# Later weight splits in a two-layer expert kernel: moving them from the step before to the first two steps of an expert

## The chip, the cores and the metric

One Trainium2 chip, one NeuronCore. The metric is the device time of one execution in microseconds, the median over several runs.

## The reference, cut to what matters

Attention over 4 batches of 576 positions gives 2304 rows of 512 numbers. Two mixture-of-experts layers follow, each with 8 experts:

```
idx  = argmax(logits, axis=1)          # one expert per row
for e in range(8):
    h = maximum(x[idx == e] @ w1[e], 0)    # 512 -> 1024
    out[idx == e] = gate[:, None] * (h @ w2[e])   # 1024 -> 512
```

Layer 0 has a normalised router with a temperature, layer 1 a plain one on the output of layer 0. The result has float32 accuracy.

## The kernel before, in words

**Steps.** The rows of one expert are gathered into tiles of 128. A layer is a row of steps `t = 0, 1, ...`, one tile each, in the order of the experts: first a large one (its first three tiles are chosen early), then the others, last another large one. Steps from 18 on run under a condition, so that only as many run as there are tiles. One step multiplies its tile with W1 (`ph0`, `ph1`, 12 matmuls each of 128 by 512), evicts, transposes, and multiplies with W2 (`py`, 24 matmuls). A tile of at most 64 rows that ends an expert of two tiles or more (from step 4 on) is a "half step" with fewer matmuls.

**Splits.** TensorE works with fp32r operands, so each weight is split into a high and a low part: ACT writes `Wh` from the staging buffer `stg` (`split_hi`, L909), DVE writes `Wl = stg - Wh` (`split_lo`, L912). A matrix is four chunks, each one operation per engine. `Wh` and `Wl` have two places per matrix: one for the current expert, one for the next. As soon as `stg` has been split, SP reloads it with the expert after the next (`loads`, `dma_chunks`, L1153 and L1155). There is one staging buffer for W1 and one for W2.

**When.** `finish2` computes with small DVE operations, for each expert with first step `s0` and `nt` tiles, the step `st` that its hand-over hangs on: `st = max(s0, 3)` for the first expert, `s0` for the others, and at least 19 for the last expert of layer 0. The next expert's W1 is split late in step `st - 1`, its W2 late in step `st`. The flags lie in two places: `ctl` holds for each step its flags (columns 4 and 5) and which expert to load (columns 0 to 3); `fw` holds the flags of 12 steps as the bits of one number, for steps 4 to 15 and 16 to 27. Steps 2 and 3 read their flags from `ctl` and the weight place from `ini`; the later ones take bits of the two words, which ACT, DVE and POOL load into registers (`words`, L1227) late in steps 2 and 14, ahead of that step's splits.

**Order in a step.** All queues are written out by hand in `step`. Late in a step come: the routing of the previous tile (layer 0, `route2`), the word loads, the splits of W2 and of W1 (L1325 is the condition, `If(self.fv[i] > 0)`), then in layer 0 `place` on DVE (L569 to L579; six tiles in steps 7 and 13, three in 16), the rest of the `py` matmuls, in the last steps of layer 0 `rank_pe`, `rank_ev` and `place` for one tile, and `end`: ACT evicts `py` into `ysb` (L1417). In `end` DVE has a condition of its own (L1426, `If(hv[0] > 0)`) under which it writes `ysb` in a half step.

**What the next step asks of these queues.** Some 3 us into a step, ACT has to evict `ph0` into `hs` (L1481), from which TensorE transposes (L1438). In layer 0, TensorE then transposes the last step's `ysb` (L1368), for which ACT and DVE must have left `end`.

Of the kernel before, what the change touches and what calls it, by code (L numbers as in the profile page):

```python
# [13 lines left out]
ALU = mybir.AluOpType  # L14
# [375 lines left out]
def tile_kernel(ctx, tc, q, k, v, M_prev, z_prev, beta, emb, tau, w1a, w2a, wg, w1b, w2b, out):  # L390
# [43 lines left out]
    k1, ntl = ctile([P, 1], "k1"), ctile([P, 1], "ntl")  # L434
    p17 = ctile([P, 1], "p17")

    TW, BW = NE + 1, 12
    pw = ctile([P, 2], "pw")
    fw = ctile([P, 2, 4], "fw", I32)

# [144 lines left out]
    class Route1:  # L585
# [62 lines left out]
        def rank_ev(self):  # L648
            V = nc.vector
            V.tensor_tensor(out=self.t8, in0=self.o, in1=self.ps, op=ALU.mult)  # L650
            yield
            V.tensor_reduce(out=rkb[:, self.sl], in_=self.t8, axis=AX.X, op=ALU.add)
            yield
# [173 lines left out]
    def finish2(L, st):  # L827
# [10 lines left out]
        ts(out=w["r2"], in0=ract, scalar1=2.0, scalar2=None, op0=ALU.add)  # L838
        ts(out=w["last"], in0=ract, scalar1=kk, scalar2=None, op0=ALU.is_ge)

        stt(out=w["st"], in0=is0, scalar=3.0, in1=s0, op0=ALU.mult, op1=ALU.max)
        V.tensor_tensor(out=c8, in0=ract.unsqueeze(1).to_broadcast([P, E, E]), in1=w["r2"].unsqueeze(2).to_broadcast([P, E, E]), op=ALU.is_equal)

        if L == 0:
# [381 lines left out]
    def words(x, engines):  # L1226
        return list(nc.values_load_multi_w_load_instructions(x, engines=engines, min_val=0, max_val=2 ** BW - 1)[1])  # L1227

    steps = {}
    flag_words, pe_words = {}, {}  # L1230

    class Step:


        def __init__(self, L, t):
            self.L, self.t = L, t
            self.hv, self.lm = None, []
            if 0 < t <= NE:
                self.pv = steps[L, 0].pv
            elif t:  # L1240
                g, k = divmod(t - TW, BW)
                self.words = flag_words[L, g]
                if (L, t) != (0, NT1 - 1):
                    self.hv = [nc.snap((self.words[3] >> k) & 1, engines=[e], min_val=0, max_val=1) for e in (DVE_, ACT_)]
            else:
                self.pv = 0 if L == 0 else nc.values_load(ini[0:1, 1, 4:5], engines=[PE_], min_val=0, max_val=1)
            self.spl = [[], []]
# [12 lines left out]
        def flags(self):  # L1260
            L = self.L
            c = ctl[self.t:self.t + 1, L]
            ld = lambda a, b, e, m: nc.values_load_multi_w_load_instructions(c[:, a:b], engines=e, min_val=0, max_val=m)[1]
            if self.t < TW:
                self.fv = ld(4, 6, [ACT_, DVE_, POOL_], 1)
                self.wv = 1 if L == 0 else nc.values_load(ini[0:1, 1, 5:6], engines=[ACT_, DVE_, POOL_], min_val=0, max_val=1)
            else:
                k = (self.t - TW) % BW
                three = [ACT_, DVE_, POOL_]
                f1, f2, pv = ((w >> k) & 1 for w in self.words[:3])  # L1270
                self.fv = [nc.snap(x, engines=three, min_val=0, max_val=1) for x in (f1, f2)]
                self.wv = nc.snap(1 - pv, engines=three, min_val=0, max_val=1)
            self.cv = ld(0, 2, [SP_], 127)
            self.ev = ld(2, 4, [SP_], E - 1)

        def gemm(self, i, ps, lhs, n0, a, b):

# [43 lines left out]
        def splits(self, i, cs, parts="hl"):  # L1321


            wv = self.wv if i else steps[self.L, self.t + 1].wv
            with tc.If(self.fv[i] > 0):  # L1325
                for c in cs:
                    for x in parts:
                        ins = (split_hi if x == "h" else split_lo)(4 * i + c, wv)
                        for y, d, g in self.spl[i]:
                            if x != y and c != d:  # L1330
                                tc.declare_no_dep(ins, group=g, reason="other chunk")
                        if i:
                            tc.declare_no_dep(ins, group=f"g{i}_{self.L}_{self.t}", reason="other buffer")
                        for mm in last_mm.get(i, ()):
                            tc.add_manual_dep(ins, mm.name, SYNC, reason="buffer free")
                        g = f"{x}{i}_{self.L}_{self.t}_{c}"
                        tc.add_to_no_dep_group(g, ins)
                        self.spl[i].append((x, c, g))
# [120 lines left out]
    def next_flags(L, t):  # L1459
        if t > 2:  # L1460
            steps[L, t].flags()

    def step(L, t):

        s, b = steps[L, t], bufs
        more = 0 < t < NS - 1
        rt2 = L == 0
        late = t >= NT1 - 2
        x = x0 if t == 0 else b.x
        lx = lambda kk: (x, kk)  # L1470
        lh = lambda kk: (b.h[kk // 4], kk % 4)
        begin(L, t)
        if s.hv is None:
            s.gemm(0, ph0, lx, 0, 0, 3)
            yield
            s.gemm(0, ph0, lx, 0, 3, 9)
            yield
            s.gemm(0, ph0, lx, 0, 9, 12)
        else:
            s.either(lambda: s.gemm(0, ph0, lx, 0, 0, 12), lambda: s.gemm2(0, ph0, lx, 0, HQ[0], True))  # L1480
        nc.scalar.activation(out=b.hs[0], in_=ph0, func=AF.Copy)  # L1481
        ahead = (L, t) != (0, NT1 - 1)
        yield
        s.either(lambda: (s.gemm(0, ph1, lx, 512, 0, 6), hT_pe(0, b)), lambda: (s.gemm2(0, ph1, lx, 512, HQ[0][0:4]), hT2_pe(0, b)))
        hT_ev(0, b, s.hv)
        if rt2:
            yT_pe()
            yT_ev(b.hs[0])
        yield
        rk = L == 0 and 2 <= t <= NT1 - 2  # L1490
        if rk:
            rank_pe(t - 2)
            rank_ev(t - 2)
        s.either(lambda: s.gemm(0, ph1, lx, 512, 6, 12), lambda: s.gemm2(0, ph1, lx, 512, HQ[0][4:], True))
        last_mm[0] = s.lm
        nc.scalar.activation(out=b.hs[1], in_=ph1, func=AF.Copy)  # L1496
        yield
        if more:
            xT_pe(rows_of(t + 1))
        if rt2:  # L1500
            parts_pe(b.hs[0])
            parts_ev(b.hs[0])
        if more:
            next_step(L, t + 1)
            hilo(psx, b.x, False, steps[L, t + 1].hv)
        if rt2:
            route2_iov()
        s.either(lambda: (s.gemm(1, py, lh, 0, 0, 3), hT_pe(1, b)), lambda: (s.gemm2(1, py, lh, 0, HQ[1][0:4]), hT2_pe(1, b)))
        hT_ev(1, b, s.hv)
        if more:  # L1510
            next_flags(L, t + 1)
        yield
        if rt2 or s.hv is None:
            s.either(lambda: s.gemm(1, py, lh, 0, 3, 6), lambda: s.gemm2(1, py, lh, 0, HQ[1][4:6]))
        gen = iter(())
        if rt2:
            logits_pe(b.hs[0])
        yield
        if s.hv is None:
            s.gemm(1, py, lh, 0, 6, 9)  # L1520
        if rt2:
            gen = route2(t - 1)
        next(gen, None)
        next(gen, None)
        drain(gen)
        if t == 2:
            s.flags()
        g, k = divmod(t + 2 - TW, BW) if t + 2 < NS else (0, 1)
        if k == 0:
            flag_words[L, g] = words(fw[0:1, g, 0:3], [ACT_, DVE_, POOL_]) + words(fw[0:1, g, 3:4], [ACT_, DVE_])  # L1530
        if not ahead:
            e2.append(nc.values_load(ini[0:1, 1, 0:1], engines=[SP_], min_val=0, max_val=E - 1))
        for i in (1, 0):
            if t > 1 + i and t < NS - 1 + i:
                s.splits(i, range(4))
                s.loads(i, range(4))
        if rk and ((t - 1) % 6 == 0 or t == NT1 - 2):
            c0 = (t - 2) // 6 * 6
            place(c0, t - 1 - c0)
        if s.hv is None:  # L1540
            for q_ in range(9, 24, 3):
                yield
                s.gemm(1, py, lh, 0, q_, q_ + 3)
        else:
            a, n = (6, 6) if rt2 else (3, 4)
            s.either(lambda: s.gemm(1, py, lh, 0, a, 24), lambda: s.gemm2(1, py, lh, 0, HQ[1][n:], True))
        if k == 0:
            pe_words[L, g] = words(fw[0:1, g, 2:4], [PE_])
        if more:
            steps[L, t + 1].pe_flags()  # L1550
        last_mm[1] = s.lm
        if (L, t) == (1, NT1 - 2):

            nc.gpsimd.drain()
        if rt2:
            nc.gpsimd.dma_start(out=x2[P * (t - 1):P * t, DM:XR], in_=xcb)
            if late:
                rank_pe(t - 1)
                rank_ev(t - 1)
                place(t - 1, 1)  # L1560
        if not ahead:

            with tc.If(rg["nt"] <= NT1):
                for c in range(8):
                    for ins in split_chunk(c, rg["wv"]):
                        tc.add_to_no_dep_group("n18", ins)
        end(L, t)

    def abreast(a, b, ns=()):

# [268 lines left out]
```

## Time and profile before

| | us |
|---|---|
| median of 3 runs (lowest to highest) | 903.15 (903.11 to 904.14) |
| the profiled execution | 903.58 |
| its span, first to last instruction | 901.9 |
| TensorE busy | 851.6 (94%) |
| DVE busy | 514.9 (57%) |
| ACT busy | 478.9 (53%) |

PE is the matmul engine TensorE, PEld its weight loads, DVE VectorE, ACT ScalarE, POOL GpSimd, SP the queue that issues most transfers. Matmuls are pipelined, so a row can say that PE is busy though the next matmul started before the last one ended. [...] In the timelines a row has: start, duration, engine, line, operation, tile written and read, shapes, how many in a row, and in brackets how long the engine sat idle before it and what ended that. Register loads, branches and semaphore waits are not rows of a timeline: they show as idle time that ends with "issue" or with a name like ACTq or DVEq (the engine's own sequencer) and a line. A step is taken from its first `ph0` matmul to that of the next.

### The profile page before, as it was taken

The page shows a single profiled execution, that of the slowest core. Times are in us where ns is not written, and L with a number is a line of the kernel's source. Part 1 is how long each engine was busy: PE and PEld are TensorE (multiplying, and loading weights), DVE is VectorE, ACT ScalarE, POOL GpSimd, SP SyncE. Part 2 cuts the span into 40 slices and gives each one's busy share as a digit, 9 for nine tenths or more (in the row PEclk, how much of TensorE's full clock was granted, in tenths as well). Part 3 has the DMA queues.
Part 4 walks back from the last instruction along what each step waited for, and adds up shares of the span by engine and source line. Part 5 has one row for each costly group of instructions (what it writes and reads, how often), then busy time and mean ns, then how long its engine had stood idle before and what let it go on. Part 6 is the DMA issues. An engine that isn't in the chain of part 4 may idle for free. (4 is left out here: it accounts for less than half of the span.)

```text
span 901.9 us, 20713 instructions
## 1 busy us (share of the span) xinstructions
PE 851.6 (94%) x5139; PEld 661.4 (73%) x5139; DVE 514.9 (57%) x1617; ACT 478.9 (53%) x940; POOL 264.0 (29%) x376
## 2 busy tenths in 40 slices
PE   5999999999999999887989999998988999989996
PEld 3777777777777777665868788776877887767785
DVE  4766676576786854676346465744467316363620
ACT  3667667667658244565344543632277426564631
POOL 5457656465451022111121112121112111111111
PEclk9999999999999999987999999999999999999998
DMA  8424454335053454366334116111659415374111
GB/s 131 80 52 95 85 153 114 58 55 113 14 174 109 173 171 150 119 232 210 124 118 144 39 35 206 69 49 39 235 179 337 156 48 181 120 271 143 44 38 40
DMA packets 139826, 110.56 MB, mean 123 GB/s; under 512 B 107258, under 2 KB 107258, under 8 KB 139652
## 3 DMA queue, kind: packets, MB, share of 16 engines
q1 hardware_dynamic: 129252, 85.03, 32.2%
q0 software_dynamic: 8032, 23.22, 7.6%
q8 instruction: 72, 1.18, 0.5%
q14 instruction: 102, 0.84, 0.3%
q10 hardware_dynamic: 2368, 0.30, 0.2%
HBM read 90.32 MB, written 19.25 MB: 121 GB/s over the span
## 5 line engine op out<-in xcount | busy, mean ns | idle before, releaser
L1312 PE MATMUL py<-Wh,b 128*128 (+1 forms) x640 | 221.1, 406 | 0.3 <-ACT hs L1496 0.3
L1312 PE MATMUL ph<-Wh,b 128*128 (+1 forms) x624 | 217.1, 405 | 0.8 <-issue 0.8
L912 DVE TENSOR_TENSOR Wl<-stg,Wh 128x1024 f32 (+1 forms) x120 | 145.7, 1225 | 33.6 <-ACT Wh L909 25.2
L1312 PEld LDWEIGHTS ph<-Wh,b 128*128 128x128 f32 x624 | 119.7, 192 | 29.1 <-issue 3.1
L1208 DVE SCALAR_TENSOR_TENSOR b<-pt,b 128x512 fp32r<-128x512 f32 (+1 forms) x86 | 56.1, 653 | 148.5 <-ACT b L1203 140.5
L1312 PEld LDWEIGHTS py<-Wh,b 128*128 128x128 f32 x640 | 120.2, 188 | 27.8 <-issue 4.7
L909 ACT ACTIVATE Wh<-stg 128x1024 f32 (+1 forms) x120 | 125.7, 1059 | 21.6 <-issue 7.7
L1312 PE MATMUL ph<-Wl,b 128*128 (+2 forms) x336 | 131.7, 398 | 0.0
L1312 PE MATMUL py<-Wl,b 128*128 (+2 forms) x344 | 128.5, 392 | 0.0
L267 ACT ACTIVATE att<-psat 128x512 f32<-128x512 f32 (+1 forms) x144 | 66.5, 462 | 76.0 <-PE psat L265 75.5
L1203 ACT ACTIVATE b<-pt 128x512 fp32r<-128x512 f32 x86 | 51.4, 598 | 85.7 <-PE pt L1438 65.5
L288 PE MATMUL psav<-vb,att 128*128 128x128 f32 (+1 forms) x640 | 93.9, 281 | 0.4 <-ACT att L267 0.2
L288 PEld LDWEIGHTS psav<-vb,att 128*128 128x128 f32 x640 | 80.3, 191 | 17.4 <-ACT att L267 5.6
L1433 POOL DMA_INDIRECT out_dram<-ysb,xca x21 | 22.7, 1083 | 203.4 <-ACT ysb L1417 83.0
L248 ACT ACTIVATE a<-a,mx 128x128 f32<-128x128 f32 (+3 forms) x128 | 71.0, 554 | 5.6 <-DVE mx L213 5.4
L1312 PEld LDWEIGHTS ph<-Wl,b 128*128 128x128 f32 (+1 forms) x336 | 62.0, 184 | 12.1
L1312 PEld LDWEIGHTS py<-Wl,b 128*128 128x128 f32 (+1 forms) x344 | 61.8, 182 | 11.6 <-ACT b L1203 1.0
L213 DVE CUSTOM_DVE_ANT_0 a<-pss,wmask 128x128 f32<-128x128 f32 (+3 forms) x128 | 60.8, 481 | 14.8 <-PE pss L235 14.2
L1438 PE MATMUL pt<-ident,hs 128*128 128x128 f32 x304 | 47.8, 281 | 16.8 <-ACT hs L1481 16.6
L1438 PEld LDWEIGHTS pt<-ident,hs 128*128 128x128 f32 x304 | 37.5, 143 | 31.0 <-ACT hs L1481 22.4
L1168 POOL DMA_INDIRECT xg<-x_scratch,idx x48 | 48.2, 1004 | 37.7 <-issue 16.2
L1417 ACT ACTIVATE ysb<-py,xca 128x512 f32<-128x512 f32 x36 | 24.6, 683 | 62.5 <-PE py L1312 50.9
(389 smaller groups left out, 1253.6 us busy)
## 6 DMA issues: line engine op xcount, KB each, us to landing
stg<-in_moe_w_dram SPq DMA_DIRECT2D x120, 512.0 KB, 8.3
x_scratch<-ysb POOLq DMA_DIRECT2D x22, 256.0 KB, 4.5
qkn<-in_q_dram SPq DMA_DIRECT2D x64, 72.0 KB, 2.4
qkn<-in_k_dram SPq DMA_DIRECT2D x60, 72.0 KB, 2.4
vb<-in_v_dram SPq DMA_DIRECT2D x32, 128.0 KB, 2.4
x_scratch<-xb SPq DMA_DIRECT2D x16, 256.0 KB, 2.9
x_scratch<-stg SPq DMA_DIRECT2D x11, 258.0 KB, 4.1
xg<-x_scratch,idx POOLq DMA_INDIRECT x48, 3.9
```

The source lines that it names most:

```text
L213: nc.vector.tensor_tensor_reduce(out=out, in0=ps, in1=mask, scale=-0.125, scalar=bound, op0=ALU.add, op1=ALU.min, accum_out=m)
L248: nc.scalar.activation(out=a[:, 0:N], in_=a[:, 0:N], func=AF.Exp, scale=-1.0, bias=mx, accum_out=rs_t[pi][:, c, j:j + 1])
L267: nc.scalar.activation(out=att[:, 0:N], in_=ps[:, 0:N], func=AF.Copy)
L288: nc.tensor.matmul(av_t[pi][:, c, j:], att[:, 128 * kb:128 * kb + 128], vn[:, kb, j:, 0:D], start=(kb == 0), stop=(kb == c))
L909: return nc.scalar.activation(out=chunk(Wh, c, wv), in_=stg[:, c].unsqueeze(1), func=AF.Copy).ins
L912: return nc.vector.tensor_tensor(out=chunk(Wl, c, wv), in0=stg[:, c].unsqueeze(1), in1=chunk(Wh, c, wv).bitcast(F32), op=ALU.subtract).ins
L1168: return nc.gpsimd.indirect_dma_start(out=rows_of(t), out_offset=None, in_=rows, in_offset=bass.IndirectOffsetOnAxis(ap=idx[:, L, t:t + 1] ...
L1203: nc.scalar.activation(out=hl[:, :, 0:P], in_=ps, func=AF.Relu if relu else AF.Copy)
L1208: nc.vector.scalar_tensor_tensor(out=o, in0=x, scalar=0.0, in1=h, op0=ALU.max, op1=ALU.subtract)
L1312: mm = nc.tensor.matmul(o, x, W, start=(first and q_ == qs[0]), stop=(last and q_ == qs[-1]))
L1417: whole = lambda: nc.scalar.activation(out=ysb, in_=py, func=AF.Copy, scale=xc[:, 0:1])
L1438: nc.tensor.transpose(pts[i][:, P * kk:P * kk + P], b.hs[i][:, P * kk:P * kk + P], ident)
```

## The change

An expert with three tiles or more gets `st = s0 + 1`: the next expert's W1 is split late in its first step, W2 late in its second, and the loads behind the splits move with them. The first expert's splits (W1 in step 2, W2 in step 3) lose their condition and their flags; the weight place is a constant in layer 0 and one register in layer 1, loaded late in step 16 of layer 0. The bit words cover steps 3 to 15 and 16 to 28, so steps 2 and 3 read no flags from `ctl`; the word loads stand behind the splits of steps 2 and 14. `end` stands ahead of the last steps' `rank_pe`, `rank_ev` and `place`. `finish2` has one DVE operation more.

```diff
-    TW, BW = NE + 1, 12
+    TW, BW = NE, 13
...
-        stt(out=w["st"], in0=is0, scalar=3.0, in1=s0, op0=ALU.mult, op1=ALU.max)
+        stt(out=w["st"], in0=nt, scalar=2.5, in1=s0, op0=ALU.is_gt, op1=ALU.add)
+        stt(out=w["st"], in0=is0, scalar=3.0, in1=w["st"], op0=ALU.mult, op1=ALU.max)
...
-            if self.t < TW:
-                self.fv = ld(4, 6, [ACT_, DVE_, POOL_], 1)
-                self.wv = 1 if L == 0 else nc.values_load(ini[0:1, 1, 5:6], engines=[ACT_, DVE_, POOL_], min_val=0, max_val=1)
-            else:
...
             self.cv = ld(0, 2, [SP_], 127)
             self.ev = ld(2, 4, [SP_], E - 1)
...
+        def split_flags(self):
+            g, k = divmod(self.t - TW, BW)
...
+            self.wv = first_wv[self.L] if self.t <= NE else nc.snap(1 - pv, engines=three, min_val=0, max_val=1)
...
-            wv = self.wv if i else steps[self.L, self.t + 1].wv
-            with tc.If(self.fv[i] > 0):
+            first = self.t == 2 + i
+            wv = first_wv[self.L] if first else self.wv if i else steps[self.L, self.t + 1].wv
+            with ExitStack() if first else tc.If(self.fv[i] > 0):
...
-        g, k = divmod(t + 2 - TW, BW) if t + 2 < NS else (0, 1)
-        if k == 0:
-            flag_words[L, g] = words(fw[0:1, g, 0:3], [ACT_, DVE_, POOL_]) + words(fw[0:1, g, 3:4], [ACT_, DVE_])
...
         for i in (1, 0):
             if t > 1 + i and t < NS - 1 + i:
                 s.splits(i, range(4))
                 s.loads(i, range(4))
+        group = {2: 0, TW + BW - 2: 1}.get(t)
+        if group is not None:
+            flag_words[L, group] = words(fw[0:1, group, 0:3], [ACT_, DVE_, POOL_]) + words(fw[0:1, group, 3:4], [ACT_, DVE_])
+        if t == 2:
+            steps[L, 3].split_flags()
+        if (L, t) == (0, NT1 - 2):
+            first_wv.append(nc.values_load(ini[0:1, 1, 5:6], engines=[ACT_, DVE_, POOL_], min_val=0, max_val=1))
...
-            if late:
-                rank_pe(t - 1)
-                rank_ev(t - 1)
-                place(t - 1, 1)
+        end(L, t)
+        if rt2 and late:
+            rank_pe(t - 1)
+            rank_ev(t - 1)
+            place(t - 1, 1)
...
-        end(L, t)
```

## Rows read from the trace of the kernel before

**Rows 1.** The page, part 5: the group of ACT's splits.

```profile
L909 ACT ACTIVATE Wh<-stg 128x1024 f32 (+1 forms) x120 | 125.7, 1059 | 21.6 <-issue 7.7
```

**Rows 2.** Stretches: steps 3, 7, 8, 9, 10, 12, 14, 15, 19 of layer 0.

```profile
326.50:341.40 14.90, 13.86 (x77) 11.08 (x77) 10.51 (x24) 10.83 (x16) 2.75 (x5) 1.00 0.54 178
...
382.50:402.80 20.30, 16.18 (x77) 12.62 (x76) 14.07 (x26) 12.56 (x17) 3.02 (x5) 0.83 0.66 235
402.80:425.40 22.60, 17.16 (x77) 13.17 (x76) 15.67 (x32) 12.64 (x17) 3.03 (x5) 0.77 0.61 210
425.40:439.10 13.70, 13.70 (x78) 11.19 (x77) 7.95 (x21) 6.06 (x10) 3.04 (x5) 1.00 0.60 195
439.10:452.70 13.60, 13.60 (x77) 11.12 (x76) 4.00 (x18) 4.33 (x8) 2.49 (x5) 1.00 0.14 42
...
463.60:481.60 18.00, 15.56 (x78) 12.26 (x77) 11.88 (x29) 10.73 (x15) 3.89 (x6) 0.91 0.43 148
...
495.20:509.20 14.00, 13.81 (x77) 10.97 (x75) 5.39 (x21) 5.06 (x9) 2.49 (x5) 1.00 0.13 40
509.20:524.40 15.20, 14.22 (x76) 11.22 (x77) 10.48 (x24) 10.38 (x15) 2.49 (x5) 1.00 0.12 38
...
566.80:581.40 14.60, 13.99 (x80) 11.07 (x79) 10.36 (x30) 8.89 (x13) 2.78 (x5) 1.00 0.13 41
```

**Rows 3.** Stretches: steps 3, 5, 7, 10, 14 of layer 1.

```profile
655.40:671.60 16.20, 14.13 (x62) 11.32 (x61) 9.61 (x10) 11.40 (x14) 3.15 (x3) 0.89 0.50 165
...
685.80:701.80 16.00, 14.17 (x61) 11.43 (x60) 12.09 (x12) 11.85 (x15) 2.21 (x3) 0.89 0.84 296
...
714.10:726.40 12.30, 12.30 (x62) 10.20 (x61) 2.07 (x3) 3.57 (x6) 2.21 (x3) 1.00 0.16 47
...
748.40:761.20 12.80, 12.78 (x61) 10.21 (x61) 9.80 (x11) 9.53 (x13) 2.21 (x3) 1.00 0.58 192
...
796.20:811.80 15.60, 12.98 (x62) 10.04 (x60) 9.86 (x11) 9.77 (x13) 2.21 (x3) 1.00 0.82 304
```

**Rows 4.** Timeline of ACT around the start of step 8, layer 0.

```profile
400.20 8.56 ACT L909 ACTIVATE Wh<-stg 128x1024 f32 x8
...
409.24 0.59 ACT L1481 ACTIVATE hs<-ph 128x512 f32<-128x512 f32 x1
```

**Rows 5.** Timeline of PE in step 8, layer 0: its two waits.

```profile
409.88 1.11 PE L1438 MATMUL pt<-ident,hs 128*128 128x128 f32 x4 [2.82 <-ACT hs L1481]
413.62 1.12 PE L1368 MATMUL pm<-ident,ysb 128*128 128x128 f32 x4 [2.62 <-DVEq L1426]
```

**Rows 6.** Timeline of ACT around the start of step 9, layer 0.

```profile
422.81 4.34 ACT L909 ACTIVATE Wh<-stg 128x1024 f32 x4
...
428.39 0.60 ACT L1481 ACTIVATE hs<-ph 128x512 f32<-128x512 f32 x1 [0.28 <-PE ph L1312]
```

**Rows 7.** Timeline of ACT: the splits late in step 11, layer 0 (a half step).

```profile
463.23 4.34 ACT L909 ACTIVATE Wh<-stg 128x1024 f32 x4 [0.27 <-ACTq L1325]
```

**Rows 8.** Timeline of DVE: splits late in step 8, `place` late in step 13, layer 0.

```profile
424.16 5.18 DVE L912 TENSOR_TENSOR Wl<-stg,Wh 128x1024 f32 x4 [0.18 <-issue]
...
494.58 0.17 DVE L569 CAST ri<-rkb 128x6 int32<-128x6 f32 x1 [0.83 <-DVEq L1325]
...
495.40 0.96 DVE L579 TENSOR_TENSOR ohp<-iop,rk 128x768 bf16<-128x768 bf16 x1
```

**Rows 9.** Timeline of PE in step 9, layer 0: the transposes of `ysb`.

```profile
429.94 0.60 PE L1368 MATMUL pm<-ident,ysb 128*128 128x128 f32 x4
```

**Rows 10.** Timeline of ACT: splits in steps 2 and 14, layer 0, and 2, layer 1.

```profile
326.82 3.91 ACT L909 ACTIVATE Wh<-stg 128x1024 fp32r<-128x1024 f32 x4 [2.85 <-issue]
...
508.48 4.34 ACT L909 ACTIVATE Wh<-stg 128x1024 f32 x4 [2.23 <-ACTq L1325]
...
656.27 4.34 ACT L909 ACTIVATE Wh<-stg 128x1024 f32 x4 [4.86 <-issue]
```

**Rows 11.** The view of the tile `stg`: time of its transfers to landing.

```profile
DMA to landing us min/median/max: 4.1/7.1/9.7
```

More of the change, by code (lines that the diff above doesn't have):

```diff
@@ L1229, in tile_kernel @@
     steps = {}
-    flag_words, pe_words = {}, {}
+    flag_words, pe_words, first_wv = {}, {}, [1]
     class Step:
@@ L1241, in __init__ @@
                 g, k = divmod(t - TW, BW)
-                self.words = flag_words[L, g]
                 if (L, t) != (0, NT1 - 1):
-                    self.hv = [nc.snap((self.words[3] >> k) & 1, engines=[e], min_val=0, max_val=1) for e in (DVE_, ACT_)]
+                    self.hv = [nc.snap((flag_words[L, g][3] >> k) & 1, engines=[e], min_val=0, max_val=1) for e in (DVE_, ACT_)]
             else:
@@ L1263, in flags @@
             ld = lambda a, b, e, m: nc.values_load_multi_w_load_instructions(c[:, a:b], engines=e, min_val=0, max_val=m)[1]
-            if self.t < TW:
-                self.fv = ld(4, 6, [ACT_, DVE_, POOL_], 1)
-                self.wv = 1 if L == 0 else nc.values_load(ini[0:1, 1, 5:6], engines=[ACT_, DVE_, POOL_], min_val=0, max_val=1)
-            else:
[L1268 to L1272, printed above, removed]
             self.cv = ld(0, 2, [SP_], 127)
             self.ev = ld(2, 4, [SP_], E - 1)
+        def split_flags(self):
+            g, k = divmod(self.t - TW, BW)
+            three = [ACT_, DVE_, POOL_]
+            f1, f2, pv = ((w >> k) & 1 for w in flag_words[self.L, g][:3])
+            self.fv = [nc.snap(x, engines=three, min_val=0, max_val=1) for x in (f1, f2)]
+            self.wv = first_wv[self.L] if self.t <= NE else nc.snap(1 - pv, engines=three, min_val=0, max_val=1)
         def gemm(self, i, ps, lhs, n0, a, b):
@@ L1461, in next_flags @@
             steps[L, t].flags()
+        if t > NE:
+            steps[L, t].split_flags()
     def step(L, t):
@@ L1546, in step @@
             s.either(lambda: s.gemm(1, py, lh, 0, a, 24), lambda: s.gemm2(1, py, lh, 0, HQ[1][n:], True))
-        if k == 0:
-            pe_words[L, g] = words(fw[0:1, g, 2:4], [PE_])
+        if group is not None:
+            pe_words[L, group] = words(fw[0:1, group, 2:4], [PE_])
         if more:
```

## The prediction

> **What bounds the kernel.** I read the page first: TensorE is busy for 94% of the span, so the question is what its steps cost above their matmuls. Its waits, longest first, name two places in the expert layers: the transposes of `hs` wait for ACT (L1481), those of `ysb` for ACT and for DVE's condition in `end` (L1426). I then cut the span at each step's first `ph0` matmul and took the stretches. Look in rows 2 and 3 for steps of equal work and unequal length. An undisturbed full step takes 13.6 in layer 0 (step 10) and 12.3 in layer 1 (step 7). Others take up to 22.6 [rows 2, 3].
>
> Which steps are long? ACT's splits are 120 operations of 1.06 us [rows 1]; on the timeline they lie four or eight at a time in the late parts of steps 2, 3, 5, 6, 7, 8, 11, 12, 14, 15, 18, 19 of layer 0 and 2, 3, 4, 5, 9, 10, 12, 13, 14, 16, 17 of layer 1 (eight in 6 and 7 of layer 0 and 3, 4 and 13 of layer 1), besides step 0. With the rule for `st` this gives the experts: first steps 0, 6, 7, 8, 12, 15, 16 in layer 0 and 0, 4, 5, 10, 13, 14, 17, 19 in layer 1. So those that the change moves are five: 8 to 11 and 12 to 14 in layer 0; 5 to 9, 10 to 12 and 14 to 16 in layer 1.
>
> A split is paid in the step after it. Eight in one step hold ACT for 8.56 us from 400.20, 2.6 before step 8 begins at 402.8; `hs` is evicted at 409.24 and TensorE waits 2.82 for it [rows 4, 5]. DVE's eight low parts and `place` then hold its queue in front of `end`, and TensorE waits another 2.62 [rows 5]. Four splits in a full step begin 2.6 before step 9 as well, but end in time: ACT waits for TensorE, `hs` is evicted 3.0 after the step's start, and step 9 takes 13.7 [rows 2, 6]. Four in a half step begin only 0.4 before the next step at 463.6, and that one takes 18.0 [rows 2, 7].
>
> **The change, part by part.** *Step 8 of layer 0.* Before, step 7 split eight; now W2 alone stays there, and W1 goes to step 8, W2 to step 9, both full steps with four splits each. By step 9 as it was, four cost the next step nothing [rows 2, 6]. But step 7 also has `place`. The four low parts take 5.18, so that DVE is done with them about 4.0 into the next step (step 8's splits: 424.16 + 5.18 is 3.9 after 425.4), `place` takes 1.8 (494.58 to 495.40 + 0.96) [rows 8], so DVE leaves `end` at 5.8. TensorE wants to transpose `ysb` at 4.5 (429.94 less 425.4) [rows 9]. I leave a wait of 1.3. Step 8: 22.6 - 13.6 - 1.3 = 7.7 saved, between 9.0 (if `place` is hidden) and 6.4 (if the wait is twice mine).
>
> *Steps 12 and 14 of layer 0.* The W1 split leaves half step 11 for full step 12, W2 goes from 12 to 13. Step 12 loses its whole excess: 18.0 - 13.6 = 4.4 [rows 2]. Step 13 has `place`, now behind a split: step 14 gains the same wait, -1.3, between 0 and -2.6.
>
> *Layer 1.* Here no `ysb` is transposed, so only ACT counts. W1 leaves step 4 for 5, so step 5 returns to 12.3: 3.7. W1 leaves half step 9 for 10: 0.5. W1 leaves step 13, which had eight, for 14: 3.3 [rows 3]. Steps 6, 11 and 15 now end with W2 splits in full steps, hidden like those of step 8 in layer 0 [rows 6]; without that cover each would cost what step 10 shows, 0.5 [rows 3].
>
> *The first expert and the flags.* In step 2 of layer 1, ACT idles 4.86 ahead of the splits [rows 10]. By the code it fetches registers: two flag pairs, twice the place, two words. Afterwards the splits can start 4.86 earlier, at 651.4, and end at 655.8; the two word loads come behind them, at most the 2.23 that they and their neighbours take in step 14 [rows 10]; `ysb` (0.7) then leaves `hs` at 657.6 to 658.7, against 658.4 wanted (3.0 into the step from 655.4). Step 3 loses its 3.9 [rows 3]. In step 2 of layer 0 the routing's last ACT operation stands between, and the idle time is 2.85 [rows 10]: splits from 324.0 to 327.9, words and `ysb` until 329.8 to 330.8, wanted at 329.5. Step 3's excess of 1.3 [rows 2] goes by between 0 and 1.3; I take 0.9. SP's two loads per step (which expert) stay where they were; POOL's word load moves behind nothing that waits on POOL.
>
> In step 14 of layer 0 the words change sides with the splits. ACT's sum stays, less what the loads overlap with the last split (up to its 1.06); DVE's wait in front of `end` goes. Step 15's excess of 1.6 [rows 2] falls by 0 to 1.6, taken as 0.8. [...]
>
> *`end` before `place`.* In steps 19 and 20 of layer 0 the one-tile `place` no longer stands in front of DVE's `end`; both have about 1.0 of excess (the row of 19 stands) [rows 2]. ACT fits, so 1.8 for the two, between 0 and 2. TensorE's own order doesn't change, since `end` gives it nothing.
>
> *Added work.* One DVE operation per layer in the chain of `finish2`, by its small neighbours 0.17 [rows 8]: 0.3. One register load in step 16, which has no splits to delay: nothing; with splits beside it, some 0.8.
>
> Sum: 7.7 + 4.4 - 1.3 + 0.9 + 0.8 + 1.8 = 14.3 in layer 0; 3.7 + 0.5 + 3.3 + 3.9 = 11.4 in layer 1; less 0.3: 25.4. The profiled execution took 903.6, so 878.2 by its measure; it stands 0.4 above the median, which gives 877.8. Untouched and late next: steps 6 and 7 of layer 0 (one-tile experts; step 7 keeps 20.3 [rows 2]) and step 4 of layer 1.
>
> **The clock in this sum.** The granted clock is 0.77 in step 8, 0.91 in 12 and 0.89 in steps 3 and 5 of layer 1, and 1.00 in the steps beside them [rows 2, 3]. [...] Each fall follows the waits I remove. [...]
>
> **Rivals.** *The clock stays* (7%): the falls have another cause and only waits go, 877.8 + 10.4 = 888.2. For it: step 3 of layer 0 has a wait and 1.00. Against: no step without a wait falls among rows 2 and 3.
>
> *The waits come back behind `place` and the words* (17%): the new splits in steps 7 and 13 make waits twice mine and each pulls the clock down as in step 12, by 1.6: 2 x (1.3 + 1.6) = 5.8, so 883.6.
>
> *More comes back* (11%): `place` hides (2.6), steps 3 and 15 lose all (1.2), and step 7's clock, 20.3 x 0.17 = 3.4, recovers: 870.6.
>
> *Other experts are picked* (3%): if the test on tile counts finds none, only flags, `end` and words remain, 3.9 + 0.9 + 0.8 + 1.8 - 0.3 = 7.1: 896.0. Against: the split steps show four, three, five, three and three tiles.
>
> *Slower, through late weights* (5%): ten groups of four transfers start a step later, and a split that finds its chunk missing holds ACT's whole queue. Between load and use lie at least two steps (W1 in step 12 and again in 14 of either layer), 24.6 us in layer 1. A transfer lands after 9.7 at most [rows 11]. It decides only if landing takes over 24.6 us; to pass 903 each of the ten must be late by 2.6 more, some 27 us to landing.
>
> **Numbers.** My forecast has 57%. The range is 871 to 887: it holds it, its bounds, and the cases of `place` and of more. A measurement of this kernel can tell about 0.2% (1.8 us) from no change. Faster by more: 0.95, all cases but the last; within it 0.02, slower 0.03, the last case split.
>
> **What would show it.** Afterwards splits lie four at a time in all steps but 6 of layer 0 and 3 of layer 1. Steps 8 and 14 of layer 0 take 13.6 to 15.0, with TensorE's wait in front of L1368 and DVE's L579 just before it; step 12 takes 13.6, steps 3, 5, 10 and 14 of layer 1 12.3, with clock 1.00. ACT's idle time ahead of the splits in step 2 of layer 1 is under 1. Wrong would be: a wait of ACT for a transfer into `stg`, a clock under 1.00 in step 8 or 12, or step 15 still at 15.2.

## The result and the profile after

| | before | after |
|---|---|---|
| median of 4 runs, us | 903.44 (903.11 to 904.14) | 876.80 (876.53 to 877.51) |
| the profiled execution | 903.58 | 876.98 |
| its span | 901.9 | 875.2 |
| mean granted clock | 0.980 | 0.992 |

The ratio is 0.9705, with a 95% interval of 0.9689 to 0.9722: 26.6 us, or 3%, less. The forecast was 877.8.

The page after: part 1 (busy time, share of the span, instructions) and, of part 5, the group of [rows 1]:

```profile
PE 839.6 (96%) x5139; PEld 655.7 (75%) x5139; DVE 515.9 (59%) x1619; ACT 479.5 (55%) x940; POOL 265.5 (30%) x377
...
L910 ACT ACTIVATE Wh<-stg 128x1024 f32 (+1 forms) x120 | 126.1, 1060 | 9.0 <-ACTq L1325 2.3
```

The same 120 splits take the same 1.06 us each. What has gone is idle time in front of them, 21.6 then and 9.0 now. Of these 12.6 us, 12.3 lie in steps 2 and 14 of both layers, where the flag and word loads stood: the three gaps of [rows 10] and a fourth of 3.09 in step 14 of layer 1. The stretches after, for steps 3, 7, 8, 12, 14, 15, 17 and 19 of layer 0 (those of [rows 2], and step 17) and 3, 5, 10 and 14 of layer 1 (those of [rows 3]). The columns, as there: the stretch in us from the span's start, its length, busy us and (x) number of instructions of PE, PEld, DVE, ACT and POOL, the granted TensorE clock as a share of full speed (before, it read 1.00 from 403.0 to 409.0 us and 0.50 from 410.0 to 418.8, so the 0.77 of step 8 is a mean), the DMA engines' share and GB/s:

```profile
325.80:339.40 13.60, 13.60 (x77) 11.12 (x76) 8.64 (x23) 7.84 (x12) 2.88 (x5) 1.00 0.56 195
...
380.50:400.80 20.30, 16.57 (x78) 12.94 (x77) 14.10 (x27) 12.65 (x17) 3.00 (x5) 0.83 0.65 235
400.80:415.80 15.00, 13.75 (x77) 11.10 (x76) 10.55 (x28) 8.22 (x13) 3.01 (x5) 1.00 0.54 177
...
454.10:467.70 13.60, 13.60 (x77) 11.12 (x76) 6.75 (x25) 6.49 (x11) 3.17 (x6) 1.00 0.14 42
...
481.30:497.00 15.70, 14.06 (x78) 10.99 (x77) 11.09 (x29) 8.94 (x13) 2.99 (x5) 1.00 0.54 169
497.00:510.70 13.70, 13.70 (x76) 11.26 (x77) 9.03 (x23) 8.28 (x13) 3.33 (x5) 1.00 0.14 43
...
524.40:540.00 15.60, 15.03 (x99) 11.90 (x99) 10.25 (x53) 4.94 (x9) 3.56 (x6) 1.00 0.21 55
...
553.70:567.40 13.70, 13.70 (x80) 11.04 (x79) 10.40 (x30) 8.86 (x13) 2.60 (x5) 1.00 0.15 44
...
640.10:652.40 12.30, 12.30 (x62) 10.20 (x61) 6.75 (x8) 7.60 (x11) 2.21 (x3) 1.00 0.60 207
...
666.60:678.90 12.30, 12.30 (x62) 10.19 (x60) 6.50 (x7) 7.33 (x10) 2.21 (x3) 1.00 0.62 210
...
725.50:737.90 12.40, 12.40 (x62) 10.28 (x62) 5.64 (x7) 6.97 (x10) 2.21 (x3) 1.00 0.11 31
...
772.70:785.70 13.00, 12.48 (x62) 10.02 (x60) 7.45 (x8) 8.29 (x11) 2.21 (x3) 1.00 0.59 201
```

Where PE's busy time equals the length, TensorE lacks nothing: steps 3, 12, 15, 19 and three of layer 1. Steps 8, 14 and 17 of layer 0 and step 14 of layer 1 have a gap, and step 7 is what it was. The two largest waits of PE in the expert steps (us in total, how many, the longest), then the rows of PE's timeline that still wait, in steps 8, 14 and 17 of layer 0 and at the start of step 15 of layer 1:

```profile
PE pt L1438 <- ACT hs L1483: 5.4, 3, 2.8
...
PE pm L1368 <- DVEq L1426: 3.4, 3, 1.3
```

```profile
406.70 0.66 PE L1368 MATMUL pm<-ident,ysb 128*128 128x128 f32 x4 [1.25 <-DVEq L1426]
...
487.27 0.65 PE L1368 MATMUL pm<-ident,ysb 128*128 128x128 f32 x4 [1.24 <-DVEq L1426]
...
525.94 0.17 PE L667 MATMUL pm<-acc,ones 128*128 128x8 bf16 x1 [0.57 <-DVE acc L1406]
...
785.65 0.50 PE L1311 MATMUL ph<-Wh,b 128*128 x1 [0.52 <-issue]
```

The 2.82 for `hs` of [rows 5] is gone from step 8; the 2.62 behind DVE's condition became 1.25. DVE's timeline says why, at the start of step 8: the first and the last row of `place`, from 4.0 us into the step until 5.8.

```profile
404.81 0.17 DVE L569 CAST ri<-rkb 128x6 int32<-128x6 f32 x1 [0.16 <-DVEq L1325]
...
405.63 0.96 DVE L579 TENSOR_TENSOR ohp<-iop,rk 128x768 bf16<-128x768 bf16 x1
```

ACT's timeline in step 2 of layer 0 and in step 2 of layer 1, where [rows 10] had 2.85 and 4.86 us of idle time in front of the splits, and of the view of L1228 (`words`) between 639 and 643 us the loads on ACT's sequencer (ns least, median and most; first and last start):

```profile
322.78 3.89 ACT L910 ACTIVATE Wh<-stg 128x1024 fp32r<-128x1024 f32 x4
...
635.99 4.33 ACT L910 ACTIVATE Wh<-stg 128x1024 f32 x4
...
641.87 0.69 ACT L1417 ACTIVATE ysb<-py,xca 128x512 f32<-128x512 f32 x1 [1.55 <-PE ph L1311]
...
L1228 ACTq TENSOR_LOAD <-fw x2: 287/503/719, 639.3 to 641.1; - x2
```

The splits have no idle time in front of them any more (no bracket). Behind those of layer 1, which end at 640.3, ACT stands idle for 1.55 us. The row puts this down to PE, but TensorE's last `py` matmul also ends at 640.3; what stands there are the word loads, the second of which begins at 641.1. Behind the splits of step 14 the same gap is 1.32 us in layer 0 and 1.39 in layer 1; in step 2 of layer 0 it is absent. It costs step 3 of layer 1 nothing: `hs` is evicted 2.9 us into the step all the same.

The span fell by 26.7. Of this 1.0 lies ahead of the expert steps, in a part that the change doesn't touch and that took 280.6 to 282.8 us over the runs below. The rest is 25.7 in the expert steps: by the sum of (1 - granted clock) x length over the steps, 17.6 us were lost to the lower clock before and 6.8 after, so 10.8 are clock, and 14.9 are waits and loads. This sum puts somewhat too much on the clock: step 6 of layer 0, with the same waits each time, took 16.5, 18.1 or 19.3 us in the runs below, 1.6 and 2.8 more, where the sum says 1.7 and 3.4. So 10.8 is too high, going by step 6 by a tenth to a fifth of it, and 14.9 is too low by as much.

### The profile page after: what moved, and what is told of

Same layout as the page of the kernel before. It is cut to its first block, busy times and chain, and to the rows that moved or that the text cites. A ratio compares the mean times of both kernels' runs of the same rounds, so it can differ in the third digit from the quotient of the medians.

```text
span 875.2 us, 20606 instructions
## 1 busy us (share of the span) xinstructions
PE 839.6 (96%) x5139; PEld 655.7 (75%) x5139; DVE 515.9 (59%) x1619; ACT 479.5 (55%) x940; POOL 265.5 (30%) x377
## 5 line engine op out<-in xcount | busy, mean ns | idle before, releaser
L1311 PE MATMUL ph<-Wh,b 128*128 (+1 forms) x624 | 213.7, 400 | 1.0 <-issue 0.9
L913 DVE TENSOR_TENSOR Wl<-stg,Wh 128x1024 f32 (+1 forms) x120 | 146.0, 1225 | 20.6 <-ACT Wh L910 12.6
L1311 PEld LDWEIGHTS ph<-Wh,b 128*128 128x128 f32 x624 | 117.7, 189 | 28.8 <-issue 3.4
L1311 PE MATMUL ph<-Wl,b 128*128 (+2 forms) x336 | 129.8, 392 | 0.0
L213 DVE CUSTOM_DVE_ANT_0 a<-pss,wmask 128x128 f32<-128x128 f32 (+3 forms) x128 | 60.8, 481 | 14.7 <-PE pss L235 13.0
L265 PE MATMUL psat<-ident,a 128*128 128x128 f32 x320 | 56.2, 276 | 0.7 <-ACT a L248 0.5
L235 PE MATMUL pss<-kT,qT 64*128 64x128 f32 (+3 forms) x256 | 55.7, 498 | 0.0
L1562 POOL DMA_DIRECT2D x_scratch<-xcb x21 | 11.9, 565 | 134.4 <-DVEq L1325 81.6
```

The costliest lines, as they stand in the source:

```text
L213: nc.vector.tensor_tensor_reduce(out=out, in0=ps, in1=mask, scale=-0.125, scalar=bound, op0=ALU.add, op1=ALU.min, accum_out=m)
L235: nc.tensor.matmul(ps[:, 0:N], qT[h, 128 * c:128 * c + 128], kT[h, 0:N], start=True, stop=True)
L265: nc.tensor.transpose(ps[:, 128 * i:128 * i + 128], x, ident)
L913: return nc.vector.tensor_tensor(out=chunk(Wl, c, wv), in0=stg[:, c].unsqueeze(1), in1=chunk(Wh, c, wv).bitcast(F32), op=ALU.subtract).ins
L1311: mm = nc.tensor.matmul(o, x, W, start=(first and q_ == qs[0]), stop=(last and q_ == qs[-1]))
```

## The experiments

Theory A: each long step is paid by the splits of the step before it, so the rule for `st` carries steps 8 and 12 of layer 0 and 5, 10 and 14 of layer 1, and the rest of the change carries 3, 15, 19 and 20 of layer 0 and 3 of layer 1; the clock follows the waits. Theory B: the clock falls for reasons of its own, and comes back only by chance. Times are medians. The kernels were run in three groups, each on one chip together with nine runs of the kernel before: the first four below (kernel before: 903.85), the next three and the version named under "The best of these" (903.66), and the last two (904.06). Ratios are to the kernel before on the same chip; where a median is set against the changed kernel's 876.8, that one was taken outside these groups.

**The rule alone**, on the kernel before:

```diff
-        stt(out=w["st"], in0=is0, scalar=3.0, in1=s0, op0=ALU.mult, op1=ALU.max)
+        stt(out=w["st"], in0=nt, scalar=2.5, in1=s0, op0=ALU.is_gt, op1=ALU.add)
+        stt(out=w["st"], in0=is0, scalar=3.0, in1=w["st"], op0=ALU.mult, op1=ALU.max)
```

> The kernel before with the rule on three tiles alone. Queue theory (a split is paid in the step after it, each removed wait counts in its own step): steps 8, 12 and 14 of layer 0 and 5, 10 and 14 of layer 1 come out as in the changed kernel (15.1, 13.6, 15.6 and 12.3, 12.3, 13.0), steps 3 of both layers and 15, 19, 20 of layer 0 as before. Differences of the stretches of the two traces: -7.5 -4.3 +1.6 -3.7 -0.5 -2.6 -0.6 (steps 13 and 15 of layer 1) = -17.6, so about 885.9 us. The clock is 1.00 in steps 8 and 12 of layer 0 and 5 of layer 1, and still 0.89 in step 3 of layer 1. Rival (the falls of the clock have another cause than the waits beside them): falls stay in steps 8, 12 or 5, 1.7 to 5.1 us more each, 888 to 895 us.

Measured: 886.19 (885.02 to 887.56), ratio 0.981 [0.9791, 0.9829]. Stretches of step 8 of layer 0 and of steps 3 and 5 of layer 1:

```profile
402.80:417.90 15.10, 13.82 (x78) 11.10 (x77) 10.61 (x28) 8.34 (x13) 3.03 (x5) 1.00 0.55 176
...
644.80:661.00 16.20, 14.13 (x62) 11.33 (x61) 9.60 (x10) 11.51 (x14) 3.16 (x3) 0.89 0.52 165
675.20:687.50 12.30, 12.30 (x61) 10.23 (x60) 7.10 (x8) 7.68 (x11) 2.22 (x3) 1.00 0.64 213
```

Step 8 and step 5 are those of the whole change; step 3, which hangs on the first expert's flags, keeps its 16.2 and its clock of 0.89. Step 15 of layer 0, expected as before, came out 0.45 shorter, at 14.7; why wasn't taken apart.

**The change without the rule**, the reverse:

```diff
-        stt(out=w["st"], in0=nt, scalar=2.5, in1=s0, op0=ALU.is_gt, op1=ALU.add)
-        stt(out=w["st"], in0=is0, scalar=3.0, in1=w["st"], op0=ALU.mult, op1=ALU.max)
+        stt(out=w["st"], in0=is0, scalar=3.0, in1=s0, op0=ALU.mult, op1=ALU.max)
```

> The changed kernel with the old rule for st: only the first expert without condition, the flags, the place of the word loads and of end remain. Queue theory: step 3 of layer 1 at 12.3 with clock 1.00 (-3.9), step 3 of layer 0 at 13.7 (-1.2), steps 15, 19 and 20 of layer 0 (-0.9 to -1.4, -0.9, -0.8), step 17 of layer 0 +0.5: -7.2 to -7.7, about 896.0 us; steps 8 and 12 of layer 0 and 5 of layer 1 as before, with clock 0.77, 0.91, 0.89. Together with the rule alone this makes -25, near the whole -26.6: the parts add up. Rival (the flags matter only where the rule has freed ACT's queue): under 3 us are gained here, above 900 us.

Measured: 894.83 (893.08 to 897.71), ratio 0.9911 [0.9887, 0.9936]. Steps 8 and 12 of layer 0, 3 and 5 of layer 1:

```profile
404.10:425.60 21.50, 15.95 (x78) 12.44 (x78) 15.67 (x32) 12.55 (x17) 3.00 (x5) 0.84 0.65 221
...
463.80:480.30 16.50, 14.06 (x78) 11.07 (x77) 11.86 (x29) 10.71 (x15) 3.90 (x6) 1.00 0.49 162
...
651.00:663.30 12.30, 12.30 (x62) 10.21 (x61) 6.75 (x8) 7.60 (x11) 2.21 (x3) 1.00 0.64 208
...
677.50:692.30 14.80, 12.81 (x61) 10.23 (x60) 11.60 (x11) 11.44 (x15) 2.22 (x3) 1.00 0.88 317
```

The two parts give 17.7 and 9.0, and their sum, 26.7, is the whole; that it fits to 0.1 is chance, for the intervals of the two ratios are about 2 us wide on either side, and the clock moved single steps of the second kernel by 1 to 2 us, as follows. Step 3 of layer 1 is undisturbed without the rule, step 8 of layer 0 isn't: A holds for the waits. Steps 12 and 5 show something that A had not: they wait as before (1.00 and 1.44 us in step 12, 1.68 in step 5 against 1.83), so they are long, but at a clock of 1.00 and not at 0.91 and 0.89, and 1.4 and 1.2 us shorter for it. Step 8, with waits of 2.78 and 2.77, ran at 0.84 and not at 0.77. There B has a point.

**`place` behind `end`**, for the wait left in steps 8 and 14:

```diff
-        if rk and ((t - 1) % 6 == 0 or t == NT1 - 2):
-            c0 = (t - 2) // 6 * 6
-            place(c0, t - 1 - c0)
...
         end(L, t)
+        if rk and ((t - 1) % 6 == 0 or t == NT1 - 2):
+            c0 = (t - 2) // 6 * 6
+            place(c0, t - 1 - c0)
```

> The changed kernel with place behind end on DVE's queue in steps 7, 13 and 16. Queue theory: in steps 8 and 14 of layer 0 TensorE waits in front of L1368 only because place stands between the low parts and DVE's condition in end; both waits (1.25 and 1.24 in the trace) go, step 8 takes 13.7 instead of 15.1 and step 14 takes 14.1 instead of 15.6: 2.9 us less, about 873.9 us. Rival (DVE's low parts themselves are late): the steps keep their lengths, 876.8 us, and the wait is put down to Wl.

Measured: 877.97 (873.67 to 879.09), ratio 0.9699 [0.9676, 0.9721]: nothing against the change's 876.8. Step 6 of the changed kernel with its two waits, then steps 6, 8 and 14 of this one:

```profile
364.00:380.50 16.50, 14.04 (x78) 11.04 (x77) 11.84 (x29) 10.67 (x15) 3.90 (x6) 1.00 0.49 161
...
369.22 0.66 PE L1438 MATMUL pt<-ident,hs 128*128 128x128 f32 x4 [1.01 <-ACT hs L1483]
371.33 0.66 PE L1368 MATMUL pm<-ident,ysb 128*128 128x128 f32 x4 [1.45 <-DVE ysb L1428]
...
365.20:384.50 19.30, 16.84 (x78) 13.01 (x76) 11.85 (x29) 10.78 (x15) 3.89 (x6) 0.82 0.42 138
...
405.30:418.90 13.60, 13.60 (x77) 11.12 (x76) 10.53 (x28) 8.19 (x13) 3.61 (x5) 1.00 0.57 195
...
484.40:498.60 14.20, 13.83 (x78) 11.00 (x76) 10.99 (x29) 8.78 (x13) 3.62 (x5) 1.00 0.56 187
```

Both steps lose their wait, 1.4 us each, as expected. So TensorE had waited there for DVE's queue to pass the condition of L1426, behind which DVE has nothing to write in a full step. But step 6, which the edit doesn't touch, took 19.3 at 0.82 where the changed kernel's took 16.5 at 1.00. The five runs of this kernel go with their mean clock: 879.1 at 0.988, 873.7 at 0.994, and 0.006 of 878 us is 5.3. So the median hides 2.9 us that the steps show.

**The words ahead of the splits again:**

```diff
+        group = {2: 0, TW + BW - 2: 1}.get(t)
+        if group is not None:
+            flag_words[L, group] = words(fw[0:1, group, 0:3], [ACT_, DVE_, POOL_]) + words(fw[0:1, group, 3:4], [ACT_, DVE_])
         for i in (1, 0):
...
-        group = {2: 0, TW + BW - 2: 1}.get(t)
-        if group is not None:
-            flag_words[L, group] = words(fw[0:1, group, 0:3], [ACT_, DVE_, POOL_]) + words(fw[0:1, group, 3:4], [ACT_, DVE_])
```

> The changed kernel with the word loads ahead of the splits of steps 2 and 14 again. Queue theory: the splits start about 2.1 later in those four steps; step 15 of layer 0 goes back to 15.1 (+1.4), step 15 of layer 1 to 12.8 (+0.4), step 3 of layer 0 by up to 1 and step 3 of layer 1 by up to 0.5: +1.8 to +3.3, 878.6 to 880.1 us. Rival (the word loads are hidden on either side): 876.8 us, and the gain of step 15 came from something else.

Measured: 880.93 (878.39 to 882.0), ratio 0.9741 [0.9722, 0.976]. Step 15 of layer 0, then steps 3 and 15 of layer 1:

```profile
500.70:515.30 14.60, 14.12 (x76) 11.15 (x77) 10.47 (x24) 10.14 (x15) 3.04 (x5) 1.00 0.13 40
...
644.50:656.80 12.30, 12.30 (x61) 10.19 (x60) 8.35 (x9) 9.19 (x12) 3.15 (x3) 1.00 0.72 218
...
790.10:802.50 12.40, 12.40 (x61) 10.31 (x62) 8.27 (x10) 9.39 (x12) 2.21 (x3) 1.00 0.63 218
```

The order of words and splits is worth 0.9 in step 15 of layer 0 and 0.1 in step 3; in layer 1 it is worth nothing, where 0.4 had been expected of step 15. So the 3.9 of step 3 in layer 1 come from the flag and place loads that are gone, not from where the words stand. The rest of the difference lies elsewhere: in the profiled execution (881.7, against 877.0) 1.6 in step 6, whose clock fell to 0.91, and 1.9 ahead of the expert steps.

**`place` twice in steps 7 and 13**, which doubles the work that is suspected of the wait:

```diff
             place(c0, t - 1 - c0)
+            if t < NT1 - 2:
+                place(c0, t - 1 - c0)
```

> The changed kernel with place issued twice in steps 7 and 13 (the second writes the same values again). Queue theory: DVE's condition in end comes 1.8 later each time, so the waits in front of L1368 in steps 8 and 14 grow from 1.25 to about 3.1, steps 16.9 and 17.4: +3.6, 880.4 us. If waits alone pull the clock down, these two steps now show it (waits of 2.8 and 2.6 did in the kernel before), 1.7 to 3.4 us more each, up to 887. Rival (DVE's low parts or the falls elsewhere set these steps): under 1 us more.

Measured: 887.74 (886.32 to 889.64), ratio 0.982 [0.9805, 0.9835]. Steps 8 and 14, and PE's wait in step 8:

```profile
403.70:423.10 19.40, 16.43 (x77) 12.93 (x76) 12.25 (x34) 8.35 (x13) 3.00 (x5) 0.82 0.40 137
...
488.90:508.90 20.00, 16.72 (x77) 12.81 (x76) 12.67 (x35) 8.94 (x13) 2.98 (x5) 0.83 0.39 133
```

```profile
411.33 1.12 PE L1368 MATMUL pm<-ident,ysb 128*128 128x128 f32 x4 [2.97 <-DVEq L1426]
```

The wait grows by 1.7, what `place` takes, and each step by 4.4: the clock fell in both, where it had been 1.00. These steps had run at 1.00 with the wait of 1.25 in all six other profiles that have it. Nothing else was put in, so here a longer wait brought the fall. This rules B out as the whole story. The median is 0.7 above the highest that was expected; step 6 fell here too, by 1.6 us.

**Two tiles instead of three:**

```diff
-        stt(out=w["st"], in0=nt, scalar=2.5, in1=s0, op0=ALU.is_gt, op1=ALU.add)
+        stt(out=w["st"], in0=nt, scalar=1.5, in1=s0, op0=ALU.is_gt, op1=ALU.add)
```

> The changed kernel with the rule at two tiles (nt > 1.5): one expert more moves, steps 17 and 18 of layer 1. Queue theory: half step 16 loses its splits, so step 17 goes from 12.95 to 12.3 (-0.65); half step 18 gets the W2 splits, so step 19 goes from 12.4 to 12.8 or 13.0 (+0.4 to +0.6): between -0.3 and 0, not to be told from 876.8 us. Rival (the fewer steps between split and use count): W2's split in step 18 comes too late for step 19, which waits in front of py, +1 to +3 us.

Measured: 880.03 (876.99 to 881.47), ratio 0.9738 [0.9718, 0.9759]. Its steps 17 and 19 of layer 1:

```profile
810.50:823.00 12.50, 12.46 (x61) 10.02 (x60) 5.17 (x7) 7.12 (x10) 2.22 (x3) 1.00 0.11 33
...
832.90:846.10 13.20, 13.02 (x61) 10.35 (x61) 7.55 (x9) 6.08 (x9) 2.22 (x3) 1.00 0.08 23
```

Step 17 gains 0.4 and step 19 loses 0.8: the two-tile expert's split only moved in front of another step. PE waited for no weight there. The rest of the difference is 1.5 in step 6, whose clock fell to 0.91, and 1.0 ahead of the expert steps.

**`end` at the very end of the step again:**

```diff
-        end(L, t)
         if rt2 and late:
...
+        end(L, t)
```

> The changed kernel with end behind rank_pe, rank_ev and place again, as in the kernel before. Queue theory: steps 19 and 20 of layer 0 go back to 14.5 (+0.85 each), step 17 keeps part of its half us (15.3 to 15.6): +1.4 to +1.7, about 878.3 us. Rival (what steps 19 and 20 gained came from the flags or the splits): steps 19 and 20 stay at 13.7, 876.8 us.

Measured: 882.98 (879.98 to 884.41), ratio 0.9762 [0.9741, 0.9783]. Its steps 17 and 19:

```profile
528.80:544.30 15.50, 15.16 (x101) 11.98 (x100) 10.23 (x53) 4.93 (x9) 3.50 (x6) 1.00 0.21 56
...
557.90:572.40 14.50, 13.90 (x78) 10.97 (x78) 10.32 (x30) 9.00 (x13) 2.49 (x5) 1.00 0.14 42
```

Steps 19 and 20 grow by 0.85 and 0.8, as expected, and step 17 loses only 0.2. The rest of this profiled execution, the slowest of the four (884.4), is 2.8 in step 6 of layer 0 and 1.4 in step 0 of layer 1, where the clock fell to 0.82 and 0.81 (1.00 and 0.90 in the changed kernel's), 1.0 ahead of the expert steps and 0.5 in step 7.

**The best of these.** `place` behind `end` in steps 7 and 13; in step 16 the old order of `place`, `rank_ev` and `end`; the weight-place register loaded in step 4. (A version with `place` behind `end` in step 16 too, 877.64 (875.42 to 879.42), missed what was expected of it: step 17 took 16.0 and not 15.1, with a wait of 1.05 us of TensorE's L719 for DVE, on whose queue by the code `place` stands in front.)

```diff
-        if (L, t) == (0, NT1 - 2):
+        if (L, t) == (0, 4):
...
-        if rk and ((t - 1) % 6 == 0 or t == NT1 - 2):
-            c0 = (t - 2) // 6 * 6
+        c0 = (t - 2) // 6 * 6
+        if rk and t == NT1 - 2:
             place(c0, t - 1 - c0)
...
-        end(L, t)
+        if t != NT1 - 2 or not rt2:
+            end(L, t)
+        if rk and (t - 1) % 6 == 0:
+            place(c0, t - 1 - c0)
...
+        if t == NT1 - 2 and rt2:
+            end(L, t)
```

> The changed kernel with place behind end in steps 7 and 13 alone, step 16 of layer 0 in the order of the kernel before (place, rank_pe, rank_ev, place, end), and the register with the weight place loaded in step 4. Queue theory: steps 8 and 14 at 13.6 and 14.2 (-2.9), step 17 at 15.1 (-0.5), steps 19 and 20 at 13.7; all steps less what the clock loses: 3.4 us under the changed kernel on the same chip, about 0.4%, though the falls of the clock in steps 6 and 7 can hide it by 1.7 to 3.4 us in a single run. Rival (step 17 waits for something else, as it did for L719 in the run with place last): step 17 at 15.6 or more, 2.9 us or less.

Measured: 874.4 (872.79 to 877.37), ratio 0.9675 [0.965, 0.97]. Steps 6, 8, 14 and 17:

```profile
365.30:383.40 18.10, 15.64 (x78) 12.07 (x77) 11.86 (x29) 10.83 (x15) 3.38 (x6) 0.91 0.45 147
...
403.90:417.50 13.60, 13.60 (x77) 11.14 (x76) 10.51 (x28) 8.17 (x13) 3.62 (x5) 1.00 0.60 195
...
483.00:497.20 14.20, 13.83 (x78) 10.99 (x76) 10.98 (x29) 8.78 (x13) 3.62 (x5) 1.00 0.56 187
...
524.60:539.70 15.10, 15.10 (x101) 11.98 (x100) 9.83 (x50) 4.93 (x9) 3.51 (x6) 1.00 0.19 56
```

**The changed kernel again**, beside it on the same chip, with no edit.

> The changed kernel itself, on this chip, beside the one above. All steps as in its first profile (877 us if the clock falls as there, 3.4 us lost in steps 6 and 7 of layer 0), up to 881 us where it falls in step 6 too. If the clock's falls are drawn anew in each execution at the same waits, its runs spread by 1.7 us and more with steps of the same length elsewhere.

Measured: 878.03 (877.0 to 880.86), ratio 0.9717 [0.9693, 0.974]. Its steps 8, 14 and 17:

```profile
404.30:419.40 15.10, 13.86 (x77) 11.14 (x76) 10.60 (x28) 8.30 (x13) 3.00 (x5) 1.00 0.57 176
...
484.90:500.50 15.60, 14.01 (x77) 10.95 (x75) 11.03 (x29) 8.85 (x13) 2.98 (x5) 1.00 0.53 170
...
528.00:543.60 15.60, 15.03 (x101) 11.91 (x99) 10.24 (x53) 4.93 (x9) 3.56 (x6) 1.00 0.24 55
```

The best version stands 3.6 us below it, and steps 8, 14 and 17 account for 1.45 + 1.45 + 0.6 = 3.5. The intervals of the two ratios still overlap by 0.0007, so by the medians alone this isn't settled; the steps carry it.

## Why the prediction was right

| step | forecast gain | measured |
|---|---|---|
| 8, layer 0 | 7.7 | 7.5 |
| 12, layer 0 | 4.4 | 4.3 |
| 14, layer 0 | -1.3 | -1.6 |
| 3, layer 0 | 0.9 | 1.2 |
| 15, layer 0 | 0.8 | 1.4 |
| 19 and 20, layer 0 | 1.8 | 1.7 |
| 5, layer 1 | 3.7 | 3.7 |
| 10, layer 1 | 0.5 | 0.5 |
| 14, layer 1 | 3.3 | 2.6 |
| 3, layer 1 | 3.9 | 3.9 |
| added work in `finish2` | -0.3 | step 2, layer 0: -0.2 |
| register load in step 16 | 0 | step 17: -0.5 |

The measured column adds up to 24.5; the other 2.2 are the 1.0 ahead of the experts, 0.7 in step 0 of layer 1 and some tenths either way elsewhere. Step 2 of layer 0 takes 14.9 with the rule alone too, and 14.7 without the rule, as before; so the 0.2 are the DVE operation's.

*Step 8.* "I leave a wait of 1.3" is 1.25 in the trace, and `place` does start 4.0 and end 5.8 into the step, as added up from rows of two steps, the splits of step 8 and the `place` of step 13. The run with `place` behind `end` shows that this wait is all that was left there; it is worth 1.45 us of the step. *Steps 12, 5, 10*: each went back to the undisturbed length, and the rule alone does it. *Steps 19 and 20* come from `end`'s place: putting it back returns 0.85 and 0.8. *Step 3 of layer 1*: the loads that no longer exist, as the runs with the words ahead and without the rule both show.

Five terms were mis-sized, none by more than 0.7. **Step 14 of layer 1**: I took its base as 12.3, but the row of PE at 785.65 shows 0.52 us of idle time ("issue") in front of the next step's first matmul, where by the code TensorE loads its own words (its queue's records of L1228 run from 783.6 on). It stood there before too:

```profile
811.80 0.49 PE L1312 MATMUL ph<-Wh,b 128*128 x1 [0.52 <-issue]
```

So the undisturbed length of this step is higher than that of its neighbours, by 0.5 of the 0.7 that were missing: the base must be taken from a step with the same extra work. **Steps 3 and 15 of layer 0**: the word loads behind the splits cost nearly nothing (step 15 is 13.7 with PE busy throughout). In step 2 of layer 0 they were fetched while the splits ran; in step 14 ACT stood idle for 1.32 us behind the splits, but `hs` was evicted 3.4 us into step 15 and TensorE didn't wait for it. My half way between the bounds was too careful, and the "more" rival was right in this one point. Of step 15's 1.4 the order of words and splits gives 0.9; the other 0.5 came with the rule alone. Where the loads ran differs: in step 2 of layer 0 ACT's two began at 322.6 and 324.3, while its splits ran from 322.8 to 326.7; in the other three steps the first began only with the last split (at 497.5 in step 14 of layer 0, at 639.3 and 784.9 in layer 1), and no run here shows why. The records of the eight word loads on ACT last 0.28 to 0.90 us, 0.49 in the median. **Step 14 of layer 0** lost 1.6 and not 1.3: its wait of 1.24 is worth 1.45, as the run with `place` behind `end` shows, and TensorE's gap at the start of step 15 ("issue") grew from 0.24 to 0.40. **The register load in step 16**, priced at nothing: TensorE's L667 waits 0.57 in step 17 for DVE, whose `place` in step 16 starts after 1.21 us of idle time on DVE, against 0.51 before:

```profile
537.42 0.17 DVE L569 CAST ri<-rkb 128x3 int32<-128x3 f32 x1 [0.51 <-DVEq L1325]
...
524.12 0.17 DVE L569 CAST ri<-rkb 128x3 int32<-128x3 f32 x1 [1.21 <-DVEq L1325]
```

Moving the load to step 4 and restoring the order of `place`, `rank_ev` and `end` in that step gave 0.6 back. Restoring `end`'s place alone gave 0.2. The rest, 0.4, is the load: in that run, which keeps it in step 16, `place` still starts 0.3 us before step 17, and in the kernel before and in the best version 0.7. So "nothing" was wrong for a queue that has `place` behind the load.

The rivals. *The clock stays* fell: in the changed kernel no step whose waits went shows less than 1.00. *The waits come back* did so at 1.25 us and no more; its condition, twice that, is the run with `place` twice, and there the clock did fall. *Other experts* fell: the split steps are those I named. *Late weights* fell: of the 9.0 us of idle time in front of the 120 splits none was ended by a transfer, and the run with two tiles, which moves loads later still, met no wait for weights either.

One thing in the sum was lucky rather than right. The 10.4 us that the first rival puts down to the clock are an estimate by [rows 2, 3], what the clock lacks of 1.00 times the length of steps 8 and 12 of layer 0 and 3 and 5 of layer 1: 22.6 x 0.23 + 18.0 x 0.09 + 16.2 x 0.11 + 16.0 x 0.11. No run shows this sum as such; step 6 shows 1.6 and 2.8 us where such a product says 1.7 and 3.4. Of the 10.4, the 3.4 of step 12 and of step 5 in layer 1 were a draw of that one execution: without the rule both waited much as before (1.00 and 1.44 us, and 1.68 against 1.83) and ran at 1.00, and were 1.4 and 1.2 us shorter for it. "Each fall follows the waits I remove" is right, but the reverse, that such waits bring a fall, isn't. Step 6 of layer 0, with waits of the same kind, ran at 1.00 in both profiled executions that were compared, so it didn't move the difference; in the ten further profiles it took 1.6 us more in six, 2.8 more (0.82) in two and nothing more in two.

## What to carry to other kernels

Price the work that one engine does late in a step by the length of the next step, and compare steps of equal work: each term here came from such a pair, to within 0.7 us. When work is moved, look up which other queue entry it now stands in front of (`place` on DVE), and take the base from a step with the same extra loads. Put register loads where nothing behind them is wanted soon: here two behind the splits cost the next step nearly nothing (step 15 of layer 0 took 13.7 us with PE busy throughout), and one in front of `place` cost 0.4 us. Where waits pull the clock down, a profile shows one draw of it: compare kernels step by step net of the clock before trusting medians that differ by less than such a fall, 1.6 or 2.8 us in step 6 here.

## What the runs showed of the hardware

The granted clock isn't a function of the waits that a profile shows. Step 6 of layer 0 has two waits of TensorE, 1.0 and 1.46 us, in all twelve profiles (before, after and ten experiments); it ran at a mean of 1.00 in four, 0.91 in six and 0.82 in two, and took 16.5, 18.1 or 19.3 us. Steps with a wait of 2.8 to 3.0 (7; 8 before and without the rule; 8 and 14 with `place` twice) fell each time; a single wait of 1.25 (8 and 14) or 1.56 (step 4 of layer 1) never did. In between it went both ways, in one execution even: before, step 5 of layer 1 fell to 0.89 with a wait of 1.83, and step 14 ran at 1.00 with one of 1.81. No run here shows what decides in a single execution. That is left open.
